# The shared key chunk's scores as float32 products in the array's quarters, issued beside the v products of the shared chunk before

## The chip, the cores and the metric

The kernel runs on one core of one Trainium2 chip. The metric is the device time of one execution in microseconds; the kernel before took 872.52 us, the median of three runs between 872.46 and 873.37.

## What is computed

```python
scale = 1.0 / np.sqrt(q.shape[-1])                       # q, k, v: (4, 12, 448, 64), float32
scores = scale * np.matmul(q, k.transpose(0, 1, 3, 2)) - np.log(S)
attn = 1.0 / (1.0 + np.exp(-scores))                     # a sigmoid, no softmax
x = np.matmul(attn, v)                                   # then laid out as 1792 tokens x 768
h = np.maximum(np.maximum(x @ w1, x @ w2), x @ w3)       # 768 x 768 each
x = h @ w_out
h = x @ w_in                                             # 768 x 2048
out = (np.maximum(h, 0) + alpha * np.minimum(h, 0)) @ w_out2
```

## The kernel before, in words

The program has three stages on one core: the attention, the first feed-forward layer (its products are the rows u and c) and the second (rows e). The change touches the attention only. Later stages are driven by the same planner and keep TensorE filled.

**The attention's unit.** Heads are taken two at a time, as 24 pairs. Head j of a pair sits on partitions 64j to 64j+63, and its 448 keys are three chunks of 128 and a rest of 64. The rests of an even pair i and the odd pair i+1 share one chunk of 128 keys, the shared chunk. Its upper half belongs to the one pair and its lower half to the other.

**Scores** (`scores`, line 551). q and k are cut into a high and a low float32r part (`cut`, lines 519 and 520, on VectorE), and a chunk is three products: high k with high q, low k with high q, high k with low q. Each product is two matmuls of 64 rows and 128 columns, one for each head, which lie in the two halves of the array's rows. For the shared chunk the tiles `kk` have 64 columns of zeros beside the keys, so `scores(i, NCH)` and `scores(i+1, NCH)` each run all six matmuls over 128 columns into the same PSUM tile: 12 matmuls. One ScalarE sigmoid (line 562) turns each finished chunk into a tile `a`. Score tiles share three PSUM slots `sc`.

**v products** (`av`, line 572). Plain float32, one matmul call for each head and chunk, and in the trace two records for each call. A full chunk uses 128 rows and 64 columns (the two heads lie in the two halves of the columns). The shared chunk's calls have 64 rows and 64 columns, and the four of them lie in the four quarters. They accumulate in `pav`, of which there are two, and ScalarE copies each finished one to `x` (`to_x`, line 595).

**The order around the change** is written out in the loop over even i. Each engine works through its own instructions in program order.

- First half, z = 0: the scores of pair i, chunks 0, 1, 2, then `rest_of(i-2)`: the shared v products of pairs i-2 and i-1, the copy of `x` for i-2, the three full chunks of pair i-1, the copy of `x` for i-1.
- Second half, z = 1: chunk 0 of pair i+1, the shared chunk (12 matmuls), chunks 1 and 2, then `first_of(i)`: the three full chunks of v products of pair i.

In each half `prep()` is called four times. It runs one of four pieces that make the next pair's q and k: `turn` k (a VectorE transpose, line 503), `cut` k (a copy and a subtraction), `turn` q, `cut` q. After each piece `advance(650)` lets the planner put out what it has ready: here the splitting of `x` for the next stage (`x_0h` by ScalarE, line 274, then `x_0l` by VectorE, line 278, and sums, line 294), and later the weights' words. The planner goes by counts of columns and calls, not by time. A piece that it emits after a `prep` call stands on its engine's queue before the next `prep` piece.

Loads of q and k (`load_pair`, line 486) are eight DMAs for each pair on SyncE's queue, two pairs ahead. Loads of v (`load_v`) are on the GpSimd queue and are issued from `turn`.

Of the kernel before, what the change touches and what calls it, by code (L numbers as in the profile page):

```python
# [9 lines left out]
F32 = mybir.dt.float32  # L10
# [3 lines left out]
AF = mybir.ActivationFunctionType  # L14
ALU = mybir.AluOpType

P = 128
# [4 lines left out]
def kernel(  # L22
# [14 lines left out]
    nc = tc.nc  # L37

    B, H, S, D = q.shape
    DM, DF1 = w1.shape[0], w1.shape[1] // 2  # L40
    DF2 = w_in.shape[1] // 2
    NCH = S // P
# [34 lines left out]
    def slot(nm, pool="a", w=TW, dt=F32):  # L77
        if pool == "a":
            pad(pool, 48)
        t = pools[pool].tile([P, w], dt, tag="s" + pool, name=nm, bufs=room[pool])  # L80
        if pool != "a":
            pad(pool, 16)
        return t
# [303 lines left out]
    def attention(apool, ps_s, ps_v):  # L387
# [9 lines left out]
            for c in range(2)  # L397
            for p in (r, r + HK)
        ]
        raw, prepped, vts, at, pv, first_k = {}, {}, {}, {}, {}, []  # L400
        kk = [
            [apool.tile([P, S + KH], F32R, tag=f"k{x}{z}", name=f"k{x}{z}") for x in "hl"]
            for z in range(2)
# [2 lines left out]
        def load_first():  # L406


            t = apool.tile([P, 2, S], F32, tag="a", name="kqn", bufs=2 * NCH + 1)
            kn, qn = (t[:, x].rearrange("p (n d) -> p n d", d=32) for x in range(2))  # L410
            for t, src, queue in ((kn, k, nc.sync), (qn, q, nc.scalar)):
                queue.dma_start(
                    out=t.rearrange("p n d -> p (n d)"),
                    in_=src[0, :2].rearrange("j (p n) d -> (j p) (n d)", p=D),
                )
            raw[0] = (qn, kn)

        def first_pair():
# [31 lines left out]
        def load_v(i, queue):  # L450
            b, p = pairs[i]
            vt = apool.tile([P, 2, NCH + 1, D], F32, tag="vt", name=f"vt{i}", bufs=4)
            if i == 0:
                n = S // D
                for j in range(2):
                    rows = v[b, 2 * p + j].rearrange("(r n) d -> r n d", n=n)
                    for x in range(2):
                        queue.dma_start(out=vt[x * D : (x + 1) * D, j, :NCH], in_=rows[:, x : n - 1 : 2])
                queue.dma_start(
                    out=vt[:KH, :, NCH],  # L460
                    in_=v[b, 2 * p : 2 * p + 2].rearrange("j (r n) d -> r j n d", n=n)[:, :, n - 1],
                )
                vts[i] = vt
                return
            k0, h0, r0 = (KH, 0, KH) if i % 2 else (0, S - KH, 0)
            for j in range(2):
                queue.dma_start(  # L467
                    out=vt[:, j, :NCH],
                    in_=v[b, 2 * p + j, k0 : k0 + NCH * P].rearrange("(c p) d -> p c d", p=P),
                )  # L470
            queue.dma_start(
                out=vt[r0 : r0 + KH, :, NCH],
                in_=v[b, 2 * p : 2 * p + 2, h0 : h0 + KH].rearrange("j p d -> p j d"),
            )
            vts[i] = vt

        def load_pair(i):
            if i >= len(pairs):
                return
            b, p = pairs[i]  # L480
            qr, kr = (slot(f"{x}{i}").rearrange("p (n d) -> p n d", d=32) for x in ("qr", "kr"))
            for t, src in ((kr, k), (qr, q)):
                for j in range(2):
                    for c in range(2):
                        p0 = 64 * j + 32 * c
                        nc.sync.dma_start(  # L486
                            out=t[p0 : p0 + 32],
                            in_=src[b, 2 * p + j, :, 32 * c : 32 * c + 32].rearrange(
                                "(n i) d -> i n d", i=32
                            ),  # L490
                        )
            raw[i] = (qr, kr)

        def prep_ops(i):

            if i >= len(pairs):
                return []
            qr, kr = raw.pop(i)
            got = {}

            def turn(which, src):
                t = slot(f"{which}t{i}")
                nc.vector.transpose(out=t, in_=src.rearrange("p n d -> p (n d)"))
                got[which] = t
                if which == "k" and 1 <= i <= 2:

                    nc.gpsimd.tensor_copy(gate[:, i : i + 1], t[:, :1])
                if which == "k":
                    for x in (i, i + 1) if i == 2 else (i,) if i != 3 else ():
                        load_v(x, nc.gpsimd)  # L510

            def cut(which, copy=nc.vector.tensor_copy):
                t = got[which]
                if which == "k":
                    k0 = KH if i % 2 else 0
                    hi, lo = (x[:, k0 : k0 + S] for x in kk[i % 2])
                else:
                    hi, lo = slot(f"qh{i}", dt=F32R), slot(f"ql{i}", dt=F32R)
                copy(hi, t)  # L519
                nc.vector.tensor_sub(lo, t, hi.bitcast(F32))  # L520
                if which == "q":
                    prepped[i] = (hi, lo)

            return [
                lambda: turn("k", kr),
                lambda: cut("k"),
                lambda: turn("q", qr),
                lambda: cut("q"),
            ]

        def scores(i, c, sc=None, stop=True):

            kh, kl = kk[i % 2]
            qh, ql = prepped[i]
            if i % 2:
                c0 = 0 if c == NCH else (c + 1) * P
            else:
                c0 = c * P
            start = sc is None
            if start:  # L540
                sc = ps_s.tile([P, 2, 512], F32, tag="sc", name=f"sc{i}_{c}")
            three = ((kh, qh), (kl, qh), (kh, ql))
            if (i, c) == (0, 0):
                kh, kl = first_k
                three = ((kh, qh), (kl, qh), (kh, ql))
            elif i == 0:
                three = ((kh, qh), (kh, ql), (kl, qh))
            for z, (kx, qx) in enumerate(three):
                for j in range(2):
                    r = slice(j * D, (j + 1) * D)  # L550
                    nc.tensor.matmul(  # L551
                        sc[:, j, :S],
                        kx[r, c0 : c0 + P],
                        qx[r],
                        start=(start and z == 0),
                        stop=(stop and z == 2),
                    )
            if stop:
                key = (i // 2, "s") if c == NCH else (i, c)
                a = apool.tile([P, 2, S], F32, tag="a", name=f"a{i}_{c}", bufs=2 * NCH + 1)  # L560
                at[key] = a
                nc.scalar.activation(a, sc[:, :, :S], AF.Sigmoid, bias=bias_s, scale=scale)  # L562
            return sc

        def av(i, c, start, stop):

# [16 lines left out]

        def rest_of(i):

            av(i, NCH, start=False, stop=True)
            av(i + 1, NCH, start=True, stop=False)
            to_x(i)
            for c in range(NCH):
                av(i + 1, c, start=False, stop=(c == NCH - 1))  # L590
            to_x(i + 1)

        def to_x(i):
            x32[i] = slot(f"x{i}")
            nc.scalar.copy(x32[i], pv.pop(i)[:, :S])
            g, r, c = i // 12, i % 12 // 4, i // 4
            form_ops(
                f"x{c}", i % 4, range(4 * c, 4 * c + 4), (g, r), xf,
                lambda g, c, r: "c" if g and r == HK - 1 else "a", lambda pool: True,
            )  # L600
# [20 lines left out]
        warm = ps_s.tile([P, 2, 512], F32, tag="sc", name="warm")  # L621
        for _ in range(6):
            nc.tensor.matmul(warm[:, 0], zeros[:, :P], zeros, start=True, stop=True)
        load_pair(1)
        for z in range(2):
            for x in kk[z]:
                nc.vector.tensor_copy(x[:, :KH] if z else x[:, S:], zeros[:, :KH])
        first_pair()
        for i in range(0, n, 2):
            for z in range(2):  # L630
# [16 lines left out]
                if z == 0:  # L647
                    for c in range(NCH):
                        scores(i, c)
                        prep()  # L650
                    if i == 0:
                        both = scores(i, NCH, stop=False)
                    prep()
                else:
                    scores(i + 1, 0)
                    prep()
                    if i:
                        both = scores(i, NCH, stop=False)
                    scores(i + 1, NCH, sc=both)
                    prep()  # L660
                    for c in range(1, NCH):
                        scores(i + 1, c)
                        prep()
# [660 lines left out]
```

## Time and profile before

| | before |
|---|---|
| median of three runs | 872.52 us |
| the profiled execution, own time | 872.05 us |
| its span, first to last instruction | 870.2 us |
| TensorE matmul busy | 862.4 us, 99% of the span |
| VectorE busy | 677.4 us, 78% |
| ScalarE busy | 527.4 us, 61% |
| chain that ended last | TensorE 98%, score products 7% and v products 8% of the span |

The profiled execution is 1.85 us longer than its span, and 0.47 us under the median of the runs. The shares are averages over three stages; the attention is the stretch from 0 to 140.7 us, and its even values of i make a cycle of about 11 us, eleven of them after the first.

### The profile page before, as it was taken

To read this page: it belongs to the slowest core of one execution; us is meant where nothing else is said; L and a number is where in the kernel's file an instruction comes from. 1 tells how busy PE (TensorE), PEld (TensorE's weight loads), DVE (VectorE), ACT (ScalarE), POOL (GpSimd) and SP (SyncE) were. 2 spreads that over 40 slices of the span, in tenths; PEclk is the share of its full clock that TensorE was granted. 3 is DMA by queue.
4 is the path that set the end of the run, shared out by engine and by line. 5 is a ranking of instruction groups with operands and counts; after the bars stand their busy time and mean duration, and the time that the engine had idled before them with its cause. 6 is when DMAs were issued, how large, how long until landed. Compare 5 with 4: busy or idle time off the path is not lost.

```text
span 870.2 us, 13603 instructions
## 1 busy us (share of the span) xinstructions
PE 862.4 (99%) x4604; PEld 746.3 (86%) x4604; DVE 677.4 (78%) x1325; ACT 527.4 (61%) x1034; POOL 146.6 (17%) x249
## 2 busy tenths in 40 slices
PE   8999999999999999999999999999999999999997
PEld 4555557999999999999999999999999999999997
DVE  5888995899879878787687877777868687768851
ACT  5888986755655554566656767667656655443430
POOL 4333330102101201300000122122221011001211
PEclk9999999999999999999999999999999999999999
DMA  7898860557655655732112443454456999445413
GB/s 150 148 184 144 171 115 14 168 154 219 202 162 172 215 147 162 231 94 73 36 53 100 136 146 132 144 179 168 144 179 196 376 325 369 136 141 164 133 50 63
DMA packets 180533, 137.00 MB, mean 157 GB/s; under 512 B 100608, under 2 KB 170368, under 8 KB 180464
## 3 DMA queue, kind: packets, MB, share of 16 engines
q1 hardware_dynamic: 163536, 93.25, 39.2%
q0 software_dynamic: 13952, 42.09, 14.2%
q10 hardware_dynamic: 2976, 0.80, 0.4%
q8 instruction: 36, 0.59, 0.3%
q14 instruction: 33, 0.27, 0.1%
HBM read 102.28 MB, written 33.82 MB: 156 GB/s over the span
## 4 chain that ended last, share of the span: by engine, by line
PE 98%; DMA 1%; SPq 1%; DVE 0%; issue 0%; DVEq 0%
PE u_0X L695 14%; PE u_1X L695 14%; PE c L695 10%; PE eW L695 10%; PE eX L695 10%; PE pav L572 8%; PE u_0W L695 7%; PE u_1W L695 7%; PE sc L551 7%; PE u_0V L695 4%; PE u_1V L695 4%; PE eV L695 3%; SPq L486 1%; DMA kr<-in_k_dram 0%; DMA qr<-in_q_dram 0%
## 5 line engine op out<-in xcount | busy, mean ns | idle before, releaser
L562 ACT ACTIVATE a<-sc,bias_s 128x896 f32<-128x896 f32 x84 | 83.0, 1020 | 13.5 <-PE sc L551 13.4
L240 ACT ACTIVATE wt<-wr 128x384 f32<-128x384 f32 x112 | 62.2, 556 | 14.8 <-DMA wr<-in_moe_w_out_dram 10.6
L572 PE MATMUL pav<-a,vt 128*64 128x448 f32 (+1 forms) x384 | 70.3, 551 | 0.0
L255 DVE CUSTOM_DVE_ANT_0 wt<-wr,wt 128x768 uint16<-128x768 uint16 x112 | 62.5, 558 | 3.9
L247 DVE SCALAR_TENSOR_TENSOR wr<-wr 128x384 uint32<-128x384 uint32 x112 | 61.9, 553 | 0.7
L725 DVE SCALAR_TENSOR_TENSOR r<-n,nalpha,r 128x448 f32<-128x448 f32 x64 | 43.4, 683 | 24.2 <-ACT n L722 24.0
L243 ACT ACTIVATE wr<-wr 128x384 uint32<-128x384 uint32 x112 | 62.0, 553 | 0.0
L758 POOL DMA_DIRECT2D gd<-r x48 | 26.0, 541 | 198.2 <-DVE r L725 196.5
L572 PEld LDWEIGHTS pav<-a,vt 128*64 128x64 f32 (+1 forms) x384 | 21.0, 135 | 38.5 <-issue 34.7
L919 POOL DMA_DIRECT2D wd<-wt x32 | 17.5, 546 | 170.3 <-DVE wt L255 157.7
L467 POOL DMA_DIRECT2D vt<-in_v_dram x46 | 35.4, 771 | 63.7 <-PE pav L572 63.3
L1166 POOL DMA_DIRECT2D out_dram<-o x28 | 17.6, 635 | 167.7 <-DVE o L1161 167.7
L246 DVE TENSOR_SCALAR wt<-wt 128x384 uint32<-128x384 uint32 x112 | 39.7, 354 | 5.5 <-ACT wt L240 5.5
L551 PE MATMUL sc<-qh,kh 64*128 64x448 f32 x192 | 37.9, 391 | 1.5 <-DVE qh L519 1.3
L828 ACT COPY u<-u_1X 128x448 f32<-128x448 f32 x34 | 18.1, 533 | 30.2 <-PE u_1X L695 30.2
L551 PE MATMUL sc<-ql,kh 64*128 64x448 f32 x192 | 35.2, 364 | 0.0
L551 PE MATMUL sc<-qh,kl 64*128 64x448 f32 x192 | 35.1, 361 | 0.0
L551 PEld LDWEIGHTS sc<-qh,kh 64*128 64x128 f32 x192 | 18.0, 183 | 19.3 <-ACT a L562 6.8
L815 ACT COPY u_0V<-u_0X 128x448 f32<-128x448 f32 x17 | 8.8, 518 | 42.1 <-PE u_0X L695 42.1
L828 ACT COPY u<-u_0X 128x448 f32<-128x448 f32 x34 | 18.1, 533 | 25.7 <-PE u_0X L695 25.4
L880 ACT COPY y<-c 128x448 f32<-128x448 f32 x24 | 12.8, 533 | 31.6 <-PE c L695 31.6
L294 DVE TENSOR_TENSOR u<-u_0W,u 128x448 f32<-128x448 f32 x28 | 17.4, 622 | 17.5 <-ACT u L828 17.0
(838 smaller groups left out, 2874.4 us busy)
## 6 DMA issues: line engine op xcount, KB each, us to landing
gl<-gd SPq DMA_DIRECT2D x79, 224.0 KB, 4.2
wr<-in_moe_w_out_dram SPq DMA_DIRECT2D x44, 384.0 KB, 4.1
wr<-in_moe_w_dram SPq DMA_DIRECT2D x36, 384.0 KB, 3.8
wr<-in_moe_w_in_dram SPq DMA_DIRECT2D x32, 384.0 KB, 3.7
wl<-wd SPq DMA_DIRECT2D x64, 192.0 KB, 4.2
gd<-r POOLq DMA_DIRECT2D x48, 224.0 KB, 2.2
gl_T<-gdT SPq DMA_DIRECT2D x32, 224.0 KB, 4.8
wd<-wt POOLq DMA_DIRECT2D x32, 192.0 KB, 4.0
```

Source lines behind the costliest of these rows:

```text
L240: nc.scalar.activation(st["T"].bitcast(F32), st["r"][:, :, 1].bitcast(F32), AF.Abs, scale=2.0**-112)
L243: nc.scalar.activation(st["r"][:, :, 0], st["r"][:, :, 0], AF.Copy, scale=2.0**-29)
L246: nc.vector.tensor_scalar(st["T"], st["T"], 3, None, ALU.logical_shift_left)
L247: nc.vector.scalar_tensor_tensor(out=st["r"][:, :, 0], in0=st["r"][:, :, 1], scalar=0x80000000, in1=st["r"][:, :, 0], op0=ALU.bitwise_and, ...
L255: nc.vector.tensor_tensor(out=st["T"], in0=st["r"][:, :, 0], in1=st["T"], op=ALU.add)
L467: queue.dma_start(out=vt[:, j, :NCH], in_=v[b, 2 * p + j, k0 : k0 + NCH * P].rearrange("(c p) d -> p c d", p=P),)
L551: nc.tensor.matmul(sc[:, j, :S], kx[r, c0 : c0 + P], qx[r], start=(start and z == 0), stop=(stop and z == 2),)
L562: nc.scalar.activation(a, sc[:, :, :S], AF.Sigmoid, bias=bias_s, scale=scale)
L572: nc.tensor.matmul(pv[i][j * D : (j + 1) * D, :S], vts[i][r, j, c, :], a[r, j, :], start=start, stop=stop,)
L695: nc.tensor.matmul(ps[:, : rh.shape[-1]], lt, rh, start=(start and z == 0), stop=(stop and z == len(mms) - 1), skip_group_check=True,)
L725: nc.vector.scalar_tensor_tensor(out=s["r"], in0=s["n"], scalar=nalpha[:, f : f + 1], in1=s["r"], op0=ALU.mult, op1=ALU.add,)
L828: nc.scalar.copy(side[g, k], banks[X][:, :TW])
```

## The change

- The shared chunk of pairs i and i+1 (i from 2 on) is no longer 12 float32r matmuls. `scores_both(i)` makes it with four float32 calls of 64 rows and 64 columns, one in each quarter of the array, from the transposed k and q themselves (`turned`), which are kept until then. The first shared chunk (i = 0) stays as it was.
- It is called inside `rest_of(i-2)`, so it stands in the first half (z = 0). There the order is now: the three full chunks of v products of pair i-1, the shared v products of i-2 and i-1, the four score calls and their sigmoid (`weigh`), and then both copies of `x`.
- The second half has chunks 0, 1, 2 of pair i+1 and `first_of(i)` only. Its four `prep` calls stay.
- The four pieces of `prep` are now `turn` k, `turn` q, `cut` k, `cut` q.
- At the start, q is loaded before k and each is split over the SyncE and ScalarE queues; three of the five first v loads go to the GpSimd queue; the loads of pair 1 come after the clearing copies, and the first waits for a VectorE copy into its tile. `load_v` is issued at other pieces for pairs 1 and 3.

```diff
-            for t, src, queue in ((kn, k, nc.sync), (qn, q, nc.scalar)):
-                queue.dma_start(
-                    out=t.rearrange("p n d -> p (n d)"),
-                    in_=src[0, :2].rearrange("j (p n) d -> (j p) (n d)", p=D),
-                )
+            for t, src in ((qn, q), (kn, k)):
+                for j, queue in enumerate((nc.sync, nc.scalar)):
+                    queue.dma_start(
+                        out=t.rearrange("p n d -> p (n d)")[j * D : (j + 1) * D],
+                        in_=src[0, j].rearrange("(p n) d -> p (n d)", p=D),
+                    )
...
+            if after is not None:
+                nc.vector.tensor_copy(kr[:, 0, :1], after[:, :1])
...
+            turned[i] = got
             return [
                 lambda: turn("k", kr),
+                lambda: turn("q", qr),
                 lambda: cut("k"),
-                lambda: turn("q", qr),
                 lambda: cut("q"),
             ]
...
+        def scores_both(i):
+            sc = ps_s.tile([P, 2, 512], F32, tag="sc", name=f"sc{i}_s")
+            for z in range(2):
+                k0 = 0 if z else S - KH
+                for j in range(2):
+                    r = slice(j * D, (j + 1) * D)
+                    nc.tensor.matmul(
+                        sc[z * KH : (z + 1) * KH, j, :S],
+                        turned[i + z]["k"][r, k0 : k0 + KH],
+                        turned[i + z]["q"][r],
+                        start=True,
+                        stop=True,
+                    )
+            weigh(sc, (i // 2, "s"), f"a{i}_s")
...
         def rest_of(i):
-            av(i, NCH, start=False, stop=True)
-            av(i + 1, NCH, start=True, stop=False)
-            to_x(i)
             for c in range(NCH):
-                av(i + 1, c, start=False, stop=(c == NCH - 1))
-            to_x(i + 1)
+                av(i + 1, c, start=(c == 0), stop=False)
+            for z in range(2):
+                av(i + z, NCH, start=False, stop=True)
+            if i + 2 < n:
+                scores_both(i + 2)
+            for z in range(2):
+                to_x(i + z)
...
-        load_pair(1)
         for z in range(2):
             for x in kk[z]:
                 nc.vector.tensor_copy(x[:, :KH] if z else x[:, S:], zeros[:, :KH])
+        load_pair(1, zeros)
...
-                    if i:
-                        both = scores(i, NCH, stop=False)
-                    scores(i + 1, NCH, sc=both)
+                    if i == 0:
+                        scores(i + 1, NCH, sc=both)
```

## Rows read from the trace of the kernel before

**Rows 1.** Windows of the attention: length, busy time by engine, clock, DMA share.

```profile
15.90:81.98 66.08, 66.08 (x482) 36.46 (x482) 53.12 (x102) 53.86 (x74) 26.57 (x38) 1.00 0.91 165
81.98:126.42 44.44, 44.33 (x322) 24.00 (x322) 43.39 (x88) 41.50 (x64) 17.23 (x24) 1.00 0.80 151
```

**Rows 2.** Chain of waits: start, length, piece, number of instructions.

```profile
15.77 0.14 issue
15.90 2.25 PE sc L551 x18
...
60.03 2.02 PE sc L551 x18
62.05 3.32 PE pav L572 x20
65.37 3.23 PE sc L551 x30
68.60 2.40 PE pav L572 x12
...
126.42 2.02 PE sc L551 x18
...
134.99 5.72 PE pav L572 x32
```

**Rows 3.** Timeline of weight loads at a shared chunk's v products.

```profile
72.96 0.21 PEld L572 LDWEIGHTS pav<-a,vt 64*64 64x64 f32 x8 [0.31 <-issue]
73.87 0.20 PEld L572 LDWEIGHTS pav<-a,vt 128*64 128x64 f32 x4 [0.70 <-issue]
74.30 0.14 PEld L572 LDWEIGHTS pav<-a,vt 128*64 128x64 f32 x2 [0.23 <-issue]
74.67 0.14 PEld L572 LDWEIGHTS pav<-a,vt 128*64 128x64 f32 x2 [0.23 <-issue]
```

**Rows 4.** Timeline of TensorE: first matmuls of the two score groups.

```profile
65.30 0.47 PE L551 MATMUL sc<-qh,kh 64*128 64x448 f32 x2
...
70.94 0.47 PE L551 MATMUL sc<-qh,kh 64*128 64x448 f32 x2
```

**Rows 5.** Timeline of ScalarE in that second half: start, length, instruction.

```profile
65.42 0.54 ACT L595 COPY x<-pav 128x448 f32<-128x448 f32 x1 [0.23 <-PE pav L572]
66.28 1.01 ACT L562 ACTIVATE a<-sc,bias_s 128x896 f32<-128x896 f32 x1 [0.32 <-PE sc L551]
67.19 0.55 ACT L274 CAST x_0h<-x 128x448 fp32r<-128x448 f32 x1
67.64 1.01 ACT L562 ACTIVATE a<-sc,bias_s 128x896 f32<-128x896 f32 x1
```

**Rows 6.** Timeline of VectorE in the same half.

```profile
66.83 0.39 DVE L519 CAST kh<-kt 128x448 fp32r<-128x448 f32 x1 [0.64 <-PE sc L551]
67.25 0.63 DVE L520 TENSOR_TENSOR kl<-kt,kh 128x448 fp32r<-128x448 f32 x1
67.80 0.62 DVE L278 TENSOR_TENSOR x_0l<-x,x_0h 128x448 fp32r<-128x448 f32 x1
68.33 0.64 DVE L503 STREAM_TRANSPOSE qt<-qr 128x448 f32<-128x448 f32 x1
69.13 0.62 DVE L278 TENSOR_TENSOR x_1l<-x,x_1h 128x448 fp32r<-128x448 f32 x1 [0.17 <-ACT x_1h L274]
69.67 0.39 DVE L519 CAST qh<-qt 128x448 fp32r<-128x448 f32 x1
```

**Rows 7.** Timeline of VectorE in the next cycle's second half.

```profile
75.11 0.63 DVE L294 TENSOR_TENSOR x_t<-x,x 128x448 f32<-128x448 f32 x1 [0.48 <-ACT x L595]
```

**Rows 8.** Timeline of the start: SyncE's queue, VectorE, TensorE.

```profile
1.21 3.64 SPq L486 DMA_DIRECT2D kr<-in_k_dram  x4
1.52 0.19 DVE L627 CAST kl<-zeros 128x64 fp32r<-128x64 bf16 x1
...
15.90 0.47 PE L551 MATMUL sc<-qh,kh 64*128 64x448 f32 x2 [1.35 <-DVE qh L519]
```

More of the change, by code (lines that the diff above doesn't have):

```diff
@@ L399, in attention @@
         ]
-        raw, prepped, vts, at, pv, first_k = {}, {}, {}, {}, {}, []
+        raw, turned, prepped, vts, at, pv, first_k = {}, {}, {}, {}, {}, {}, []
         kk = [
@@ L456, in load_v @@
                     rows = v[b, 2 * p + j].rearrange("(r n) d -> r n d", n=n)
+                    if j:
+                        queue = nc.gpsimd
                     for x in range(2):
@@ L475, in load_v, with load_pair @@
             vts[i] = vt
-        def load_pair(i):
+        def load_pair(i, after=None):
             if i >= len(pairs):
@@ L504, in turn @@
                 got[which] = t
[L505 to L510, printed above, removed]
+                if which == ("k" if i > 1 else "q"):
+                    if i <= 3:
+                        nc.gpsimd.tensor_copy(gate[:, i : i + 1], t[:, :1])
+                    load_v(i, nc.gpsimd)
             def cut(which, copy=nc.vector.tensor_copy):
@@ L558, in scores, with weigh @@
             if stop:
[L559 to L562, printed above, removed]
-            return sc
+                weigh(sc, (i // 2, "s") if c == NCH else (i, c), f"a{i}_{c}")
+            return sc
+        def scores_both(i):
[12 more added lines that the diff above has]
+            weigh(sc, (i // 2, "s"), f"a{i}_s")
+        def weigh(sc, key, nm):
+            a = at[key] = apool.tile([P, 2, S], F32, tag="a", name=nm, bufs=2 * NCH + 1)
+            nc.scalar.activation(a, sc[:, :, :S], AF.Sigmoid, bias=bias_s, scale=scale)
         def av(i, c, start, stop):
```

## The prediction, made before the change was run

> **What bounds the kernel now.** I read the chain of waits first. It lies on TensorE nearly throughout, and in the attention each cycle has the same four pieces: 2.02 us of scores (pair i, 18 matmuls), 3.32 of v products, 3.23 of scores (pair i+1 and the shared chunk, 30 matmuls), 2.40 of v products; together 10.97 [rows 2]. The reader is to see there that no other engine ends a wait in a steady cycle. The windows come next: TensorE is busy in all of the 66.08 us of the first six cycles, VectorE in 53.12 and ScalarE in 53.86; in the next four cycles, where the first weights are prepared too, VectorE is busy in 43.39 of 44.44 us and ScalarE in 41.50 [rows 1]. So TensorE sets the pace, but both helpers are close behind, and how close can't be read from shares. For that I read the order of one second half (i = 10) on three engines.
>
> Call C the start of that half's first score matmul (65.30), and A the start of the next first half (70.94), which is C+5.64 [rows 4]. ScalarE copies `x` at C+0.12, starts the sigmoid of chunk 0 at C+0.98 and the cast `x_0h` at C+1.89 [rows 5]. VectorE begins cut k at C+1.53, where it waited for TensorE to be done with the old k tile (the shared chunk's matmuls read it), and then does `x_0l`, turn q, `x_1l`, and `qh` from C+4.37 to C+4.76 [rows 6]. Group A needs `qh` and starts 0.14 us after it when it has to wait for it (the issue piece ahead of 15.90) [rows 2]. The margin of this half is therefore 5.64 - 4.90 = 0.74 us. This is the number on which the forecast turns.
>
> **The change part by part.**
>
> *TensorE's work.* The 12 matmuls that go are the difference of the two score pieces, 3.23 - 2.02 = 1.21 us [rows 2]. The float32 calls that come are not in the trace, but v products of the same shape are: their eight weight loads start at 72.96 and the next shape's at 73.87, so 0.91 us for four calls of two records [rows 3]. The steady step of two records that overlap is 74.30 to 74.67, 0.37 [rows 3], so two more rounds in four quarters take 0.75 behind work of the same shape, and the joint group 1.66. The full chunks of that piece take 3.32 - 0.91 = 2.41. Bounds for the new four calls: 0.75, since eight records in four quarters can't be fewer than two rounds, to 3.0 if no two overlap. I take 0.75, the row of the same shape. By TensorE alone the first half lasts 2.02 + 2.41 + 1.66 = 6.09 (before 5.34) and the second 2.02 + 2.40 = 4.42 (before 5.64): a cycle of 10.51, which is 0.46 less.
>
> *What stands behind C on ScalarE.* Before, one copy of `x` (C+0.12) preceded the second half's first sigmoid. Now the shared sigmoid stands first in the queue, since its scores end where C begins, then two copies, and only then the sigmoid of chunk 0. With 0.91 from a sigmoid to the next instruction and 0.45 from a cast or copy of this width to the next [rows 5]: shared sigmoid C+0.12, copies C+1.03 and C+1.48, sigmoid C+1.93, `x_0h` C+2.84. It was C+1.89, so it is 0.95 later.
>
> *What waits for it on VectorE.* `x_0l` comes out after the second `prep` call, as before. That call now runs turn q, so cut k and cut q both stand behind `x_0l` on VectorE's queue, where cut k stood ahead of it. `x_0l` starts 0.61 after `x_0h` (67.19 to 67.80): C+3.45. Then with the steps of [rows 6]: `kh` +0.53 = C+3.98, `kl` +0.42 = C+4.40, `x_1l` +0.55 = C+4.95, `qh` +0.54 = C+5.49, ended after 0.39 at C+5.88, and group A starts at C+6.02. TensorE is done with the second half at C+4.42, so it stands still for 1.60 us. The old wait for the k tile is gone (its last reader is now in the first half), but what is late next is worse: 1.9 us later at `x_0l`.
>
> In every second cycle the first product is another one: `x_t` waits for the copy of `x` (it waited 0.48 already) [rows 7]. Now that copy is the one at C+1.03, done at about C+1.6; behind it stand turn q and a sum, and then `x_6l`, whose ScalarE half is again at C+2.84. From there the order and the sum are the same, C+6.02.
>
> *The first half then.* A group that began on a wait for `qh` took 2.25 instead of 2.02, as `ql` comes late too [rows 2, 8]. So A to C is 2.25 + 2.41 + 1.66 = 6.32 by the chain, whose pieces start 0.07 after the first matmul (65.37 against 65.30) [rows 2, 4]: 6.25. In that time VectorE has one pair's four pieces and up to five others, which fit; I add nothing. One cycle: 6.02 + 6.25 = 12.27 against 10.97, so 1.30 longer.
>
> *The sum.* From 15.90 to 126.42 there are ten cycles, 110.52 us [rows 2]. Now ten of 12.27 make 122.7; in the four dense ones weight words stand between the splits, some of their ScalarE halves older, and I take off 0.5 in all (bounds: nothing, and 4 x 1.6 = 6.4 if they stall not at all). That is 122.2, or +11.7. The last cycle has no next pair to prepare: from 126.42 to the end of 134.99 + 5.72 it takes 14.29 now, and then 2.25 + 2.41 + 1.66 + 2.02 + (5.72 - 0.91 - 0.15) + 0.91 = 13.9, -0.4 (0.15 for the one change of shape that its v products save: 0.91 less 0.75).
>
> *The start.* Pair 1's loads were issued from 1.21 and now stand behind the four casts that end at 1.71, but three v loads leave the queues that they share; the first four issues took 3.64 with a wait in them [rows 8]. Turn q now comes before cut k, so from landing to `qh` cut k's 0.97 (0.42 + 0.55) is added when q is late. At best the whole idle 1.35 ahead of 15.90 goes, at worst the loads' delay of 0.7 stays. I take -0.3.
>
> *Costed at nothing.* The transposed tiles are kept until the end of the first half, so loads that reuse their space may start only then. Eight issues at 3.64 for four are 7.3 us at most, within a cycle of 12.27; were that cover gone, a late load would add its own lateness to turn k. The later load_v calls are covered in the same way: v is used a cycle after. The stages after the attention start later by the same amount and do the same.
>
> Against the profiled execution: 872.05 + 11.7 - 0.4 - 0.3 = 883.05. The median of the runs lies 0.47 above that execution: 883.5.
>
> **The rivals.**
>
> *Faster: TensorE keeps the pace.* It needs `qh` to end by C+4.42 - 0.14 = C+4.28. For it: the old wait on the k tile goes, VectorE has 13 us free in the first six cycles [rows 1], and if nothing between turn k and `qh` waited for ScalarE it would be in time. Against it: the written order. Then ten cycles give -4.6, the last -0.6, the start -0.3: 867.0. This is where it ends on the other side.
>
> *The helpers' totals.* The Trainium skill's page TensorEngine Tiling (Array Packing), section PSUM Bottleneck, says that packing speeds up TensorE but not the emptying of PSUM, which may become the bound. As a mechanism of this kernel: in the four dense cycles VectorE's 43.39 busy us exceed 4 x 10.51 = 42.04, so they gain 1.05 and not 1.84, while ScalarE's 41.50 stay below [rows 1]: 867.8. Against it as the whole story: totals leave out in which order the two engines wait for each other.
>
> *A half hold.* If the planner puts `x_0l` out one call later, behind cut k, then `x_0l` C+3.45, `x_1l` C+3.98, `qh` C+4.52 to 4.91, A at C+5.05: a cycle of 11.3, +0.3, near 875. Break-even is at A = C+4.7. Against it: the call count is unchanged.
>
> *The quarters don't overlap in pairs:* +0.75 in each of 11 cycles on top, near 892. Against it: the four v calls in 0.91 [rows 3].
>
> *Loads or space late as well:* 1 to 5 us on top, 884 to 888. For it: only that the kept tiles shrink the room.
>
> **How the numbers follow.** Forecast 0.75 (its own range 878 to 887: the ten cycles 0.5 us shorter or 0.4 longer), half hold 0.07, no overlap 0.04, loads 0.03, the two faster cases 0.11 together. What a measurement can tell from no change is 0.2%, 1.7 us. Slower: 0.75 + 0.05 of the half hold + 0.04 + 0.03, 0.87, of which I put 0.02 down to slips in this working: 0.85. Faster 0.12, same 0.03. The range 874 to 888 holds the forecast, the half hold and the late loads.
>
> **What would show it.** Right: 16 weight loads of 64 by 64 in 1.66 us; TensorE idle about 1.6 us ahead of each first half, released by `qh`; VectorE idle about 2 us ahead of `x_0l` or `x_6l`, released by ScalarE; cycles near 12.3. Wrong: cycles near 10.5 without that idle time (the first rival), or `qh` early and the wait at the new score calls.

## The result

The changed kernel takes 885.38 us, the median of four runs between 884.53 and 886.24, against 872.53 for the kernel before beside it: a ratio of 1.0144 with an interval of 1.0132 to 1.0156. The forecast was 883.5, slower. The profiled execution took 886.24 us.

TensorE's share of the span fell from 99% to 97%, though it was given less work. The page after, its first part, over a span of 884.5 us (busy us, share of the span, instructions):

```profile
PE 861.6 (97%) x4560; PEld 737.8 (83%) x4560; DVE 675.3 (76%) x1326; ACT 526.6 (60%) x1034; POOL 148.6 (17%) x253
```

The chain of waits after, one cycle. Where [rows 2] show four TensorE pieces, ScalarE and VectorE now stand between 75.28 and 80.38:

```profile
68.09 2.25 PE sc L557 x18
70.35 3.32 PE pav L595 x20
73.67 0.75 PE sc_s L575 x8
74.42 0.82 PE sc L557 x6
75.28 0.17 issue
75.45 0.60 ACT x L620 x2
76.13 0.16 issue
76.29 1.03 ACT a L586
77.32 0.46 ACT x_0h L274
77.84 0.51 issue
78.35 0.40 DVE kh L524
78.77 0.63 DVE kl L525
79.39 0.54 DVE x_1l L278
79.93 0.31 DVE qh L524
80.24 0.14 issue
80.38 1.66 PE sc L557 x11
```

Of the same half three timelines, first TensorE's (it answers to [rows 4]; the bracket is the idle time before the instruction and what ended it). C is 74.35 and A is 80.38, C+6.03:

```profile
72.68 0.98 PE L595 MATMUL pav<-a_s,vt 64*64 64x448 f32 x8
73.48 0.93 PE L575 MATMUL sc_s<-qt,kt 64*64 64x448 f32 x8
74.35 0.47 PE L557 MATMUL sc<-qh,kh 64*128 64x448 f32 x2
...
80.38 0.47 PE L557 MATMUL sc<-qh,kh 64*128 64x448 f32 x2 [1.49 <-DVE qh L524]
```

ScalarE's (against [rows 5]): the shared sigmoid `a_s` stands ahead of the copies, and `x_0h` starts at C+2.84:

```profile
74.54 1.01 ACT L586 ACTIVATE a_s<-sc_s,bias_s 128x896 f32<-128x896 f32 x1 [1.14 <-PE sc_s L575]
75.45 0.96 ACT L620 COPY x<-pav 128x448 f32<-128x448 f32 x2
76.29 1.03 ACT L586 ACTIVATE a<-sc,bias_s 128x896 f32<-128x896 f32 x1
77.19 0.58 ACT L274 CAST x_0h<-x 128x448 fp32r<-128x448 f32 x1
```

VectorE's (against [rows 6]): 2.42 us of waiting ahead of `x_0l`, with `kh`, `kl` and `qh`, whose data had long been there, behind it:

```profile
77.81 0.63 DVE L278 TENSOR_TENSOR x_0l<-x,x_0h 128x448 fp32r<-128x448 f32 x1 [2.42 <-ACT x_0h L274]
78.35 0.39 DVE L524 CAST kh<-kt 128x448 fp32r<-128x448 f32 x1
78.77 0.63 DVE L525 TENSOR_TENSOR kl<-kt,kh 128x448 fp32r<-128x448 f32 x1
79.31 0.62 DVE L278 TENSOR_TENSOR x_1l<-x,x_1h 128x448 fp32r<-128x448 f32 x1
79.84 0.39 DVE L524 CAST qh<-qt 128x448 fp32r<-128x448 f32 x1
```

The windows give the size. Five cycles, then the rest up to the last; columns as in [rows 1]. In the first TensorE is idle for 7.54 us, 1.5 in each cycle, where it was never idle before:

```profile
31.17:92.69 61.52, 53.98 (x380) 25.77 (x381) 43.95 (x87) 44.86 (x62) 21.23 (x30) 1.00 0.80 146
...
92.69:140.85 48.16, 43.29 (x305) 20.65 (x305) 42.78 (x88) 41.65 (x64) 17.04 (x24) 1.00 0.65 130
```

At the start there is something that the forecast did not have. TensorE's timeline at the second pair's first scores (they answer to the last line of [rows 8]), then the windows around it; the third number from the end is the granted clock:

```profile
17.33 0.47 PE L557 MATMUL sc<-qh,kh 64*128 64x448 f32 x2 [2.70 <-DVE qh L524]
...
18.21 0.57 PE L557 MATMUL sc<-qh,kh 64*128 64x448 f32 x2
18.58 0.57 PE L557 MATMUL sc<-qh,kl 64*128 64x448 f32 x2
```

```profile
17.00:18.00 1.00, 0.67 (x6) 0.43 (x6) 0.96 (x3) 0.00 (x0) 0.00 (x0) 1.00 0.64 103
18.00:19.00 1.00, 1.00 (x9) 0.89 (x10) 0.77 (x2) 0.49 (x1) 0.49 (x2) 0.60 0.72 116
19.00:20.00 1.00, 1.00 (x8) 0.91 (x6) 0.96 (x3) 0.89 (x2) 1.00 (x2) 0.50 0.65 106
```

TensorE started 1.43 us later than before, after a pause of 2.70 instead of 1.35, and from some 18.2 to some 21.6 us its granted clock was 0.50, the lower of its two levels (1.2 GHz). That half lasted 7.81 us where the others last 6.25. The mean granted clock of the four executions says how often it happened: 0.997, 0.998 and 0.997 in three, 1.000 in the fastest (884.53 us).

The sum in the two profiled executions, from the starts of the groups: start +1.43; from there to the last cycle 123.52 against 110.45 us, of which the slow clock is 1.56 and the ten cycles +11.51; last cycle 13.86 against 14.29, -0.43. The attention's end moves from 140.64 to 154.71, +14.07, and the span by 14.3.

### The profile page after: what moved, and what is told of

Read it like the earlier page. It is cut to its first block, busy times and chain, and to the rows that moved or that the text cites. A ratio compares the mean times of both kernels' runs of the same rounds, so it can differ in the third digit from the quotient of the medians.

```text
span 884.5 us, 13554 instructions
## 1 busy us (share of the span) xinstructions
PE 861.6 (97%) x4560; PEld 737.8 (83%) x4560; DVE 675.3 (76%) x1326; ACT 526.6 (60%) x1034; POOL 148.6 (17%) x253
## 4 chain that ended last, share of the span: by engine, by line
PE 88%; DVE 4%; ACT 2%; DMA 2%; SPq 2%; issue 1%; ACTq 0%; DVEq 0%
PE u_0X L719 14%; PE u_1X L719 14%; PE c L719 10%; PE eW L719 10%; PE eX L719 10%; PE u_1W L719 7%; PE u_0W L719 7%; PE u_0V L719 3%; PE u_1V L719 3%; PE eV L719 3%; PE pav L595 3%; PE sc L557 3%; SPq L492 1%; DMA qr<-in_q_dram 1%; ACT a L586 1%
## 5 line engine op out<-in xcount | busy, mean ns | idle before, releaser
L586 ACT ACTIVATE a<-sc,bias_s 128x896 f32<-128x896 f32 x73 | 72.1, 1022 | 15.5 <-PE sc L557 15.3
L595 PE MATMUL pav<-a,vt 128*64 128x448 f32 (+1 forms) x296 | 60.6, 551 | 0.0
L557 PE MATMUL sc<-qh,kh 64*128 64x448 f32 x148 | 30.8, 410 | 16.6 <-DVE qh L524 16.6
L595 PEld LDWEIGHTS pav<-a,vt 128*64 128x64 f32 (+1 forms) x296 | 19.0, 138 | 31.0 <-issue 25.7
L557 PEld LDWEIGHTS sc<-qh,kh 64*128 64x128 f32 x148 | 14.3, 186 | 35.6 <-ACT a L586 13.8
L852 ACT COPY u<-u_0X 128x448 f32<-128x448 f32 x34 | 18.2, 534 | 25.4 <-PE u_0X L719 25.0
L557 PE MATMUL sc<-ql,kh 64*128 64x448 f32 x148 | 28.7, 384 | 0.1
L294 DVE TENSOR_TENSOR u<-u_1W,u 128x448 f32<-128x448 f32 x28 | 17.5, 624 | 13.7 <-ACT u L852 9.1
```

Source lines behind the costliest of these rows:

```text
L557: nc.tensor.matmul(sc[:, j, :S], kx[r, c0 : c0 + P], qx[r], start=(start and z == 0), stop=(stop and z == 2),)
L595: nc.tensor.matmul(pv[i][j * D : (j + 1) * D, :S], vts[i][r, j, c, :], a[r, j, :], start=start, stop=stop,)
L852: nc.scalar.copy(side[g, k], banks[X][:, :TW])
```

## Experiments

The theory: both helpers work strictly in their written order. ScalarE's shared sigmoid delays `x_0h`, VectorE waits for it at `x_0l`, and the pieces of k and q behind `x_0l` are late for the next pair's scores (the queue). Here, as in the forecast, C is the start of a second half's scores and A that of the next first half's. Rivals: the float32 products themselves cost time; TensorE waits for PSUM slots that ScalarE empties late; the start carries the loss. Verdicts are against the kernel before, run beside each.

**1. The float32 products alone, at their old place** (on the kernel before).

```diff
...
-                        both = scores(i, NCH, stop=False)
-                    scores(i + 1, NCH, sc=both)
+                        scores_both(i)
+                    else:
+                        scores(i + 1, NCH, sc=both)
```

> The kernel before, with one part of the change alone: the shared chunk from i = 2 on is made by the four float32 calls in the quarters, at the old place in the second half; order of the pieces, of the v products and the copies, and the start are the old ones. TensorE then changes shape twice more in each cycle: scores 6 matmuls 0.8 us, quarters 0.91, scores 12 matmuls 1.42, together 3.13 instead of 3.23. Theory (queue): the products themselves cost nothing, cycles near 10.9, the old k tile is free earlier for VectorE; 870 to 872.5 us. Rival (the float32 products are dear): cycles of 11.5 or more, 878 and above.

Measured 871.85 us (871.44 to 872.7), ratio 0.9991 [0.9982, 1.0001]. The cycle is 10.87 us against 10.97. VectorE waits for `x_0l` in this kernel too, but with both pieces of k ahead of it, and the chain of waits stays on TensorE:

```profile
68.18 0.62 DVE L278 TENSOR_TENSOR x_0l<-x,x_0h 128x448 fp32r<-128x448 f32 x1 [0.73 <-ACT x_0h L274]
```

Twelve matmuls of three terms and eight float32 records are nearly the same to TensorE in this place. The loss is in what was moved and reordered with them, not in the products.

**2. k cut before q is turned, as before the change; the rest as changed.**

```diff
                 lambda: turn("k", kr),
-                lambda: turn("q", qr),
                 lambda: cut("k"),
+                lambda: turn("q", qr),
                 lambda: cut("q"),
```

> The changed kernel with the four pieces of prep in the old order: turn k, cut k, turn q, cut q. Theory (queue): in each second half VectorE's pieces stand behind a split of x whose ScalarE half comes only after the shared sigmoid and two copies (C+2.84). With cut k ahead of that split, x_0l still starts at C+3.45, and behind it stand turn q, x_1l and qh: qh ends at C+5.47, the next first half starts near C+5.61 instead of C+6.03, so a cycle is 0.42 us shorter: about 4 us in all, 1 more at the start, near 880 us (878 to 882). Rival (order alone, ScalarE has no part in it): the idle time goes, cycles near 10.5 to 10.9, 867 to 871 us. Rival (the loss is made at the start, where TensorE ran at half clock for 3.4 us): cycles stay at 12.28, about 884.

Measured 880.63 us (880.41 to 881.2), ratio 1.0092 [1.0077, 1.0107]. C to A is 5.59 and 5.83 us by turns instead of 6.03; A to C stays at 6.25. `x_0l` still starts at C+3.45, but behind it stands turn q instead of the two pieces of cut k. In every second half (the 5.83) the first product is `x_t`, which waits for the copy of `x`, and cut k still stands behind that; the expectation of 0.42 in every cycle missed it. Over ten cycles the gain is 3.0 us; the other 2.9 us of the 5.8 between the two profiled executions are the start: second pair at 15.94, and the clock at 1.00.

**3. Two pieces per call in the second half's first calls, so that both cuts stand ahead of `x_0l`.**

```diff
-                    if ops:
-                        ops.pop(0)()
+                    for _ in range(2 if z else 1):
+                        if ops:
+                            ops.pop(0)()
                     advance(650)
```

> The changed kernel, but in each second half the four pieces run in the first two prep calls, two in each, so that cut k and cut q stand ahead of the split of x on VectorE's queue; the planner is called as often as before. Theory (queue): TensorE's idle time ahead of each first half goes; the light cycles come to 10.5 us, the dense ones to 10.5 to 11 (VectorE is busy for 10.85 of them), the start with its slow stretch stays: 868 to 873 us. Rival (ScalarE itself is the bound by its total, or PSUM slots of the scores): a new wait on ScalarE takes the place, 876 or more. Rival (float32 products in quarters cost more than they save): no better than 882.

Measured 873.05 us (871.47 to 875.02), ratio 1.0006 [0.9996, 1.0015]: just above the queue theory's range. C to A is 4.48 in every cycle, so TensorE no longer waits for `qh`; the queue theory holds for that wait. But A to C is now 6.15 or about 7.0 by turns, and the mean cycle is 11.0. TensorE's third chunk of such a half, and ScalarE ahead of it:

```profile
84.08 0.47 PE L557 MATMUL sc<-qh,kh 64*128 64x448 f32 x2 [0.60 <-ACT a L586]
```

```profile
77.72 1.01 ACT L586 ACTIVATE a_s<-sc_s,bias_s 128x896 f32<-128x896 f32 x1 [2.46 <-PE sc_s L575]
78.62 0.96 ACT L620 COPY x<-pav 128x448 f32<-128x448 f32 x2
...
81.28 1.03 ACT L586 ACTIVATE a<-sc,bias_s 128x896 f32<-128x896 f32 x1
82.55 0.57 ACT L274 CAST x_4h<-x 128x448 fp32r<-128x448 f32 x1 [0.23 <-DVE x L294]
83.02 1.90 ACT L586 ACTIVATE a<-sc,bias_s 128x896 f32<-128x896 f32 x2
```

So the score-slot rival is true one step later. The Trainium skill's page TensorEngine Tiling (Array Packing), section PSUM Bottleneck, says that emptying PSUM can become the bound. Here it ends a wait (0.60 us), but not by ScalarE's total, since ScalarE stood idle for 2.46 us ahead of the shared sigmoid: the slot is emptied by the first of the two sigmoids at 83.02, and from 77.72 to 82.3 ScalarE works without a break through what stands ahead of it. A further 0.23 us is ScalarE's wait at `x_4h` for VectorE's sum, which stands behind the cuts that were moved ahead.

**4. The copies of `x` ahead of the shared scores, so ahead of their sigmoid on ScalarE.**

```diff
-            if i + 2 < n:
-                scores_both(i + 2)
             for z in range(2):
                 to_x(i + z)
+            if i + 2 < n:
+                scores_both(i + 2)
```

> The changed kernel with both copies of x ahead of the shared scores and their sigmoid; nothing else. Theory (queue): ScalarE makes the two copies while TensorE still does the shared scores, so the shared sigmoid, the first sigmoid of the half and x_0h come about 0.85 us earlier, x_0l at C+2.6 instead of C+3.45, the next first half at C+5.2: cycles near 11.4, 876 to 879 us. Rival (order of the pieces alone): cycles stay at 12.28, 885. Rival (start): 885.

Measured 879.76 us (877.98 to 880.27), ratio 1.0078 [1.0063, 1.0093], a little above the range. `x_0h` starts 2.00 us after C instead of 2.84, and C to A falls from 6.03 to 5.35, not by the whole 0.85: `kh` behind `x_0l` takes 0.55 here instead of 0.39. The cycle is 11.60, and the slow clock at the start was there again (0.50 from 19 to 21 us).

**5. Edits 3 and 4 together, with the start as changed and with the loads of before.**

> The changed kernel with the two pieces of preparation per call in the second half's first calls, and both copies of x ahead of the shared float32 scores and their sigmoid in ScalarE's order. With the pieces alone C to A was 4.48 us and A to C 6.15 or about 7.0 by turns, because the first half's third chunk waited for ScalarE's sigmoid. Theory (ScalarE is behind by the shared sigmoid, and a chain of slots passes it on): the copies and the x split start about 0.85 us earlier, VectorE is idle less, C to A stays at 4.5, and the wait of up to 0.85 us in every second cycle goes wholly or in part: cycle 10.5 to 10.8, total 866.5 to 870. Rival (ScalarE's work between the same two points is unchanged, so the same sigmoids are late whatever stands first): A to C keeps its alternation, cycle 11.0, total 872 to 874.

> Both edits of the run before and the loads of the start as before the change. If the start's loads cost 1 us or more apart from the clock, 1 to 1.5 us below the run before (865 to 869); if they cost only through the clock, and the clock stays at 1.00 in both, the same within 0.5 us.

Measured 869.96 us (869.09 to 871.93), ratio 0.9972 [0.9962, 0.9983], and 870.48 us (869.19 to 871.05), ratio 0.9971 [0.9961, 0.9982]. Both are faster than the kernel before by 0.3% and 15 us faster than the change as it was made. The chain of the first is TensorE alone again, with the pieces that the forecast gave for TensorE by itself:

```profile
24.49 0.75 PE sc_s L575 x8
25.24 2.09 PE sc L557 x18
27.33 2.41 PE pav L595 x12
29.74 2.02 PE sc L557 x18
```

C to A is 4.50 and A to C 6.09, so 10.58 a cycle, except in three of the ten, whose second half is 0.5 to 0.7 us longer because its third chunk waits for the slot that the shared sigmoid empties. The first of the three begins with a late load: VectorE waited for q, so its sum, ScalarE's `x_5h` (idle for 1.56 us) and the copies and shared sigmoid behind that came late.

```profile
64.45 0.65 DVE L509 STREAM_TRANSPOSE qt<-qr 128x448 f32<-128x448 f32 x1 [1.69 <-DMA qr<-in_q_dram]
```

In the other two, at 83.37 to 94.41 and 94.41 to 105.55 us, where the first weights are prepared too, ScalarE was busy for 10.91 of 11.04 and 11.14 of 11.14 us, so there its total is the bound or close to it. The rival's alternation is gone; the ten cycles take 107.93 us in the second of the two. The loads of the start make no difference in the medians.

**6. The loads of the start as before the change; the rest as changed.**

```diff
-            for t, src in ((qn, q), (kn, k)):
-                for j, queue in enumerate((nc.sync, nc.scalar)):
...
+            for t, src, queue in ((kn, k, nc.sync), (qn, q, nc.scalar)):
...
-                    if j:
-                        queue = nc.gpsimd
...
+        load_pair(1)
         for z in range(2):
...
-        load_pair(1, zeros)
```

> The changed kernel with the loads of its start put back as before the change (the first pair's raw q and k in one load each, the first v on one queue, the second pair's loads issued before the zeroing copies); the moved float32 scores and everything in the cycles as changed. In the changed kernel the second pair's first score matmul starts at 17.33 us after 2.70 us of waiting, and the granted clock stands at 0.50 until 21.56; before, 15.90 after 1.35 us at clock 1.00. If the loads are the cause of the late start: start at 15.9 to 16.4, pause under 2 us, no fall of the clock, total 882.0 to 883.2 (3.0 us or somewhat less gained). If the order of the preparation (turn k, turn q, cut k, cut q) is: one more turn of about 0.5 us stands before the first cut, the pause stays over 2 us, the clock falls again, total 884 to 886. The cycles stay at 12.28 us in either.

Measured 885.3 us (884.66 to 886.69), ratio 1.0147 [1.0133, 1.0161], no different from the change. In the profiled execution the second pair started at 17.13 us after a pause of 2.00, and the clock stayed at 1.00; so neither theory fits whole. The loads aren't shown to be the cause: turn q began at 15.03 us, against 15.23 in the changed kernel. What differs by the order is the way from there to the scores. VectorE at the start of the changed kernel, and with k cut early (edit 2):

```profile
15.23 0.65 DVE L509 STREAM_TRANSPOSE qt<-qr 128x448 f32<-128x448 f32 x1 [3.07 <-DMA qr<-in_q_dram]
15.80 0.35 DVE L524 CAST kh<-kt 128x448 fp32r<-128x448 f32 x1
16.25 0.62 DVE L525 TENSOR_TENSOR kl<-kt,kh 128x448 fp32r<-128x448 f32 x1
16.80 0.39 DVE L524 CAST qh<-qt 128x448 fp32r<-128x448 f32 x1
```

```profile
14.72 0.65 DVE L509 STREAM_TRANSPOSE qt<-qr 128x448 f32<-128x448 f32 x1 [1.47 <-DMA qr<-in_q_dram]
15.40 0.40 DVE L524 CAST qh<-qt 128x448 fp32r<-128x448 f32 x1
```

From turn q to the first matmul it is 2.10 us (15.23 to 17.33) with cut k between, and 1.22 (14.72 to 15.94) without: 0.88. It is 2.0 to 2.1 in all eight profiles with this order and 1.2 to 1.3 in all five with the other. When turn q begins varies from 14.28 to 15.53 us over these profiles, with no regard to the version; what makes it vary was not tested.

**7. TensorE kept at work in the pause, and the changed kernel again beside it.**

```diff
-        def scores(i, c, sc=None, stop=True):
+        def scores(i, c, sc=None, stop=True, fresh=False):
...
-            start = sc is None
-            if start:
+            start = sc is None or fresh
+            if sc is None:
...
                     for c in range(NCH):
-                        scores(i, c)
+                        fed = None
+                        if (i, c) == (2, 0):
+                            fed = ps_s.tile([P, 2, 512], F32, tag="sc", name="fed")
+                            for _ in range(6):
+                                nc.tensor.matmul(fed[:, 0], zeros[:, :P], zeros, start=True, stop=True)
+                        scores(i, c, sc=fed, fresh=True)
```

> The changed kernel with six bf16 matmuls on zeros (128x512, some 0.22 us each at full clock) given to TensorE between the first pair's last score matmul and the second pair's first, into the score slot that is used next, which is overwritten. They fill a part of the pause of 2.70 us; the data of the second pair comes no earlier. Theory (the pause brings the clock down, and the slow clock costs 1.56 us of the start in the profiled execution): clock 1.00 throughout, the second pair's start still at 17.0 to 17.6 us, its first half 6.25 us long instead of 7.81, profiled execution 884.5 to 884.9, median 0.5 to 1.2 us below the changed kernel's beside it. Rival (the clock falls for another reason, such as the start's load on the array): clock at 0.50 near 18 to 21 us as before, no gain.

> The changed kernel as it is, beside the run before, so that the two medians stand on the same chip: 885.2 to 885.6, its executions between 884.5 and 886.3 with the clock down at the start in some of them.

Measured 884.36 us (883.83 to 884.94) against 885.82 (885.44 to 886.72) without the filling: 1.46 us less, and no execution of the one reaches the other's. The 885.82 lies a little above its own expectation, 885.2 to 885.6. The mean granted clock was 0.999 or 1.000 in the four executions with the filling, 0.997 or 0.998 in the five without. The profiled execution took 884.28. The second pair started at 16.87 us, since q landed sooner; its first half lasted 6.34 us at a clock of 1.00. TensorE of this kernel (one of the six filling matmuls has no record), then the windows of the pause and the half:

```profile
14.83 1.46 PE L678 MATMUL fed<-zeros 128*128 128x512 bf16 x5
16.87 0.47 PE L557 MATMUL fed<-qh,kh 64*128 64x448 f32 x2 [0.58 <-DVE qh L524]
```

```profile
14.83:16.87 2.04, 1.40 (x5) 0.48 (x6) 1.87 (x5) 1.75 (x2) 0.00 (x0) 1.00 0.85 153
16.87:23.21 6.34, 6.34 (x46) 2.81 (x46) 4.19 (x8) 2.80 (x3) 2.79 (x5) 1.00 0.81 145
```

Without it, the changed kernel's clock fell again in its profiled execution: the second pair started at 17.14, and its first half lasted 7.55 us. So the slow clock comes of the pause. Of the 1.48 us between the two profiled executions 1.21 is that half, the top of the range given (0.5 to 1.2); the other 0.27 is the earlier start, for the most part q's landing (turn q at 14.86 against 15.04).

**8. Edits 2, 3 and 4 together, with either start.**

> The changed kernel with the pieces two per call, the copies of x ahead of the shared sigmoid, and k cut before q is turned (the order of before the change). The run without this last edit started its second pair at 17.5 us or later, after a pause of TensorE of over 2 us, and its granted clock stood at 0.50 from 18 to 20 us; with the early cut alone the start was at 15.94 and the clock stayed at 1.00. Theory (the order of the preparation makes the late start and with it the slow clock): start at 16.0 to 16.5, clock 1.00 throughout, cycles unchanged at 10.5 to 10.8, total 1.0 to 2.5 us below the run without it: 867 to 869. Rival (the start's lateness is the transfer's: q's last load lands at about 15 us in any order): start at 17, total 869.5 to 871.

> The same three edits and the loads of the start as before the change. By the order theory the loads make no difference: 867 to 869, within 0.7 us of the run beside it. If the loads count, 1 us or more lower.

Measured 870.02 us (869.13 to 871.87), ratio 0.9973 [0.9962, 0.9984], and 869.92 us (869.38 to 871.13), ratio 0.9969 [0.9959, 0.998]. The expected gain of 1.0 to 2.5 us over edits 3 and 4 alone didn't come. In the profiled execution of the first it is there (second pair at 15.76, clock 1.00, attention ended at 137.53 us against 140.53), but it stands against the slowest of the seven executions of edits 3 and 4 (871.93); in that of the second, q's turn began at 15.25, the pause was 2.23 us and the clock fell although k was cut early. The medians of the four versions with edits 3 and 4 lie within 0.6 us of each other, and the executions of each spread over 1.75 to 2.84. That the order is worth its 0.88 us there is not shown by the times; why the spread hides it stays open.

## Why the prediction was right, and which term was mis-sized

| step of the forecast | forecast | measured |
|---|---|---|
| joint group of v products and float32 scores | 1.66 | 1.67 (72.68 to 74.35) |
| `x_0h` | C+2.84 | C+2.84 |
| `x_0l` | C+3.45 | C+3.46 |
| `kh`, `kl` | C+3.98, C+4.40 | C+4.00, C+4.42 |
| `x_1l`, `qh` | C+4.95, C+5.49 | C+4.96, C+5.49 |
| next first half A | C+6.02 | C+6.03 |
| A to C | 6.25 | 6.25 |
| ten cycles, clock apart | 122.2 | 121.96 |
| last cycle | 13.9 | 13.86 |
| start | -0.3 | +1.43, and 1.56 by the clock |

*The cycle.* Walking the written order of each engine with durations of rows from before gave every step to 0.02 us, since the order, the durations and the hand-over times did not change, only which piece stood behind which. Experiments 2 to 4 each took one link of that chain out, and C to A moved by that link: 0.2 to 0.4, 1.55 and 0.68 us. The signs came as named: TensorE idle for 1.49 us (1.6 forecast), VectorE for 2.42 ahead of `x_0l`, and in every second cycle for some 3.9 ahead of `x_t` (not of `x_6l`). One reading in the forecast is wrong, the "1.9 us later at `x_0l`": C+3.45 against C+2.50 before is 0.95; nothing in the sum uses it.

*Dense cycles.* The 0.5 us taken off for them was 0.84 in the trace, 10 x 12.28 less 121.96 (one C to A was 5.12).

*The rivals.* TensorE keeping the pace at 867.0 was ruled out by the order, and the kernel comes near it when the order is mended: 869.96 in experiment 5, 10.58 us in most cycles against the forecast 10.51 for TensorE alone. What is left of the 3 us is, in the profile with the loads of before, the start (+1.49 against -0.3) and the ten cycles (-2.5 against -4.6). The helpers' totals did not bind in the changed kernel; in the mended one ScalarE's is the bound or close to it in two of the ten cycles, where the forecast had looked to VectorE's. The quarters do overlap in pairs, the forecast's 0.75 for the new calls is the chain's 0.75. Space and loads of later pairs were not late in the changed kernel: after the second pair's first half VectorE waited for one once, 0.41 us at 118.78, and no half grew by it. In the shorter cycles of experiment 5 one load was late by 1.69 us and cost up to 0.7.

*The start: the term that was wrong.* The step was "Turn q now comes before cut k, so from landing to `qh` cut k's 0.97 is added when q is late", followed by -0.3 as the value taken. Its own 0.97 measured 0.88 (experiment 6), but it was left out of the sum on the hope of an earlier q, and the +1.43 that came lies outside the bounds the term was given (-1.35 to +0.7). Of the +1.43, 0.67 is q, which was not earlier (turn q began at 15.23 against 14.56 before), and 0.76 the longer way from turn q to the scores (2.10 against 1.34). The 0.67 is chance as far as is known: over the profiles that time spreads by 1.25 us. And the longer pause brought the slow clock, which nothing in the forecast allowed for. The profiled execution lies 3.2 us above its forecast of 883.05, and start and clock together are 3.3 above theirs (1.43 + 1.56 + 0.3). The median is only 1.9 above, and that is partly luck: the forecast put the median 0.47 above the profiled execution, and it came 0.86 below it, the profiled one being the slowest of the four.

## What to carry to other kernels

When work moves from one half of a cycle to another, list each helper engine's instructions in their written order around the move and walk the times forward; shares of busy time (ScalarE 60%, VectorE 76%) say nothing of a piece that waits behind a neighbour for data of its own that is there. A move that TensorE's work alone makes worth 0.46 us a cycle cost 1.3 here, and gave 0.3% once the pieces with ready data were put ahead of those that wait, and the copies ahead of the sigmoid that nobody needs soon. A wait at the start of a kernel is to be priced with what it does to TensorE's clock, not by its length alone.

## What the runs showed of the hardware

The pause ahead of the second pair and the granted clock after it, over the profiled executions:

| version | TensorE idle before, us | clock after |
|---|---|---|
| changed kernel, two profiles | 2.70, 2.15 | 0.50 |
| edit 4 | 2.51 | 0.50 |
| edits 3 and 4 | 2.27 | 0.50 |
| edits 2, 3 and 4, loads of before | 2.23 | 0.50 |
| changed, loads of before | 2.00 | 1.00 |
| edits 3 and 4, loads of before | 1.85 | 1.00 |
| products alone; kernel before; edit 3 | 1.42; 1.35; 1.10 | 1.00 |
| edit 2; edits 2, 3 and 4 | 0.94; 0.57 | 1.00 |

At 0.50 the score matmuls followed each other every 0.37 us instead of 0.20, for about 3 us. The pauses of some 1.5 us in each cycle of the changed kernel never brought the clock down: 1.00 in the windows from 31.17 us on.
